# The first two rows of wo loaded by three DMAs over 100, 20 and 8 partitions

## The chip, the cores and the metric

The kernel runs on one core of one Trainium2 chip. The metric is the device time of one execution in microseconds, as the median over several runs. The inputs lie in HBM; a core has five engines (TensorE, called PE in the profile, VectorE or DVE, ScalarE or ACT, GpSimd or POOL, and SyncE or SP), an on-chip memory of 128 partitions, and 16 DMA engines, which carry every load.

## The reference

The reference mixes two branches for four tokens (B = 4, one position each) by a gate.

```python
g = _sigmoid((x * gate_w).sum(-1, keepdims=True))        # x: 4 x 1 x 512
# branch A: attention over the last 4096 of 16384 cached positions
q = (x @ wq) as 32 heads of 128
scores = einsum(q, k) * 128 ** -0.5                      # 8 key heads, each used by 4 query heads
p = softmax(scores)
a = einsum(p, v).reshape(B, 1, 4096) @ wo                # wo: 4096 x 512
# branch B: a gated unit
b = einsum(relu(x @ W_gate) * (x @ W_up), W_down)        # 512 x 1792, 512 x 1792, 1792 x 512
out = g * a + (1 - g) * b
```

All inputs are bf16. Keys and values of the window are 8 sets of 4 MB each, wq and wo 4 MB each, and the three matrices of branch B 1.75 MB each.

## The kernel before

The kernel doesn't call its engines one by one. It first collects, in a `Program` (lines 28 to 172), a list of operations for each engine, each with the names of the operations that it waits for, and then emits each list in the order in which it was collected. `Program.dma` (line 56) adds a DMA: unless a semaphore is named, each DMA gets one of its own, and its event is the count 16 on it. An operation waits for an event by waiting until the semaphore has reached the event's count.

Nearly all loads are issued by SP, in one queue and in this order: wq (line 568), then the key sets and value sets in turn (`load_k` at line 263, `load_v` at line 267), the two matrices W_gate and W_up (lines 279 and 280), the last value set, W_down (line 282), and last wo (lines 284 to 289). ACT issues two tiny loads at the start, x and gate_w (lines 273 and 274): they go to 16 and 4 partitions of the tile `xs`, and both have an outermost size of 4 in the source.

wo is seen as 128 partitions x 32 rows x 512 columns: a partition holds 32 consecutive rows of wo, 1 KB each. It goes to the tile `Wo`, which is another view of the memory `KT` that holds the transposed keys; so its DMAs wait for the last matmul that reads the keys, `("SC", NSET - 1, 1)`. `WO_CUTS = (0, 18, 26, 30, 32)` (line 23) cuts the 32 rows of a partition into four pieces of 18, 8, 4 and 2 rows, that is 2304, 1024, 512 and 256 KB, each loaded over all 128 partitions by one DMA with a semaphore of its own, `("WO", k)`.

The attention runs over 8 sets (a token and half of its key heads each), in a loop that PE executes once a set: scores, the maximum, the exponent, a permutation, the transposition of the weights, and the product with the values. Branch B's products are done in the last turn. Behind the loop stands the tail (lines 514 to 556):

- 14 matmuls of the "grouped" kind (`grouped`, line 516) multiply branch B's hidden values with W_down. They work in four groups of 32 PE columns in turn and add up into the tile `SB`.
- The last set's attention output is normalised and transposed; in the meantime PE does 4 and then 8 matmuls whose result nobody reads (`unread`, line 523, `IDLE = (4, 8)`).
- The rows 0 to 17 of each partition of wo (`GROUPED = 18`) go through 18 more grouped matmuls (line 533), each waiting for its piece of wo and for the attention output `oq`. ACT copies the sum to `part` (line 536).
- The rows 18 to 31 go through four matmuls each, one for a quarter of the columns (line 540), into the tile `AB`; each waits for its piece. After the first of these pieces, the matmuls of line 549 add `part` in.
- DVE and ACT copy the quarters to `outr` (line 554), and SP stores the result (line 574).

Of the kernel before, what the change touches and what calls it, by code (L numbers as in the profile page):

```python
# [15 lines left out]
NSET = 8  # L16
# [3 lines left out]
FAR = 1.0e9  # L20
LOWEST = -3.0e38

WO_CUTS = (0, 18, 26, 30, 32)
IDLE = (4, 8)
GROUPED = 18

# [148 lines left out]
def bass_gated_mix__sliding_block_cached__glu_gated_reglu__decode_kernel(  # L175
# [13 lines left out]
    with ExitStack() as ctx:  # L189
        def sb(name, shape, dt):  # L190
            return ctx.enter_context(nc.sbuf_tensor(name, shape, dt))
# [33 lines left out]
        p = sb("p", [128, 512], BF16)  # L225
# [26 lines left out]
        Wo = KT[:, :].bitcast(BF16).rearrange("p (i w) -> p i w", w=512)  # L252
# [3 lines left out]
        P = Program()  # L256
# [25 lines left out]
        P.dma("sp", lambda e: e.dma_start(Wd[:, :, :].rearrange("p i w -> p (i w)"),  # L282
                                          B_W_down.rearrange("(p i) w -> p (i w)", p=128)), ("WD",))
        wo_src = A_wo.rearrange("(p i) w -> p i w", p=128)
        for k in range(len(WO_CUTS) - 1):
            lo, hi = WO_CUTS[k], WO_CUTS[k + 1]
            P.dma("sp", lambda e, lo=lo, hi=hi: e.dma_start(  # L287
                Wo[:, lo:hi, :].rearrange("p i w -> p (i w)"),
                wo_src[:, lo:hi, :].rearrange("p i w -> p (i w)")), ("WO", k), [("SC", NSET - 1, 1)])

        P.op("pool", lambda e: e.memset(xz[:, :, :].rearrange("p t w -> p (t w)"), 0.0), ("XZ0",))
        P.op("pool", lambda e: e.memset(onesf[:, :], 1.0), ("ONESF",))
# [223 lines left out]
        def grouped(n, stat, mov, waits):  # L516
            g = n % 4
            P.op("pe", lambda e: e.matmul(SB[32 * g:32 * g + 32, :], stat, mov, start=(n < 4), stop=(n >= total - 4),
                                          tile_position=(0, 32 * g)), ("GR",) if n == total - 1 else None, waits)
# [13 lines left out]
        for i in range(GROUPED):  # L533
            k = max(k for k in range(len(WO_CUTS)) if WO_CUTS[k] <= i)
            grouped(NFT + i, oq[:, i:i + 31 * 32 + 1:32], Wo[:, i, :], [("WO", k), ("OQ",)])
        P.op("act", lambda e: e.copy(part[:, :], SB[:, :]), ("PART",), [("GR",)], sem="va")
        def quarter(q):
            return AB[32 * q:32 * q + 4, 128 * q:128 * q + 128]

        for k in range(1, len(WO_CUTS) - 1):  # L540
            for i in range(WO_CUTS[k], WO_CUTS[k + 1]):
                for q in range(4):
                    P.op("pe", lambda e, i=i, q=q: e.matmul(  # L543
                        quarter(q), oq[:, i:i + 97:32], Wo[:, i, 128 * q:128 * q + 128],
                        start=(i == GROUPED), stop=(i == 31), tile_position=(0, 32 * q)),
                        ("ACC",) if (i == 31 and q == 3) else None, [("WO", k), ("OQ",)])
            if k == 1:
                for q in range(4):
                    P.op("pe", lambda e, q=q: e.matmul(quarter(q), S32[:, 0:4], part[:, 128 * q:128 * q + 128],
                                                       start=False, stop=False, tile_position=(0, 32 * q)), None,  # L550
                         [("PART",), ("S32",)])
        for q in range(4):
# [3 lines left out]
                sem="fin" if q % 2 else None)  # L556
# [63 lines left out]
```

## Time and profile before

| what | value |
|---|---|
| median of 3 runs | 196.72 us (196.71 to 197.96) |
| the profiled execution's own time | 197.05 us |
| its span, first to last instruction | 195.5 us |
| mean granted TensorE clock | 0.769 |
| read from HBM | 81.01 MB, 414 GB/s over the span |
| the four pieces of wo, issue to landing | 20.8, 22.9, 23.6, 23.8 us |

The profile is that of one execution, and its times are microseconds from the start of the span. The 40 digits of a slice row are tenths of busy time in 40 equal slices of the span, some 4.9 us each; the DMA row is the mean over the 16 DMA engines. The chain is the work that ended last, followed back from the last instruction: "DMA KT<-in_A_wo_dram" is a time in which the chain waited for that load. In a timeline a line is: start, duration, engine, line of the kernel, operation, what it writes and reads, how many, and in brackets the idle time of its engine before and what ended that. In the view by windows a row is: the stretch, its length, the busy time of each engine with the number of instructions, the granted clock, the busy share of the DMA engines, and GB/s. "SPq" is the queue of DMAs that SP issues. In the rows for DMA queues, q1 is SP's queue and q10 is ACT's; each has its number of packets, MB, and share of the 16 engines' time.

### The profile page before, as it was taken

How to read it: one execution, taken by the hardware profiler on the slowest of the kernel's cores; microseconds unless marked ns; L12 is line 12 of the kernel's file. 1: busy time of each engine (PE TensorE's matmuls, PEld its weight loads, DVE VectorE, ACT ScalarE, POOL GpSimd, SP SyncE). 2: the span in 40 equal slices, each digit the busy share in tenths (PEclk: the TensorE clock that was granted, in tenths of full speed). 3: DMA queues.
4: the chain of work that ended last, by engine and by line, in shares of the span. 5: the costliest groups of instructions: out<-in, count | busy, mean ns of one | idle time of the engine just before them, and what ended most of it. 6: DMA issues, size and time to landing. Idle time of an engine off the chain costs nothing.

```text
span 195.5 us, 2431 instructions
## 1 busy us (share of the span) xinstructions
PE 94.6 (48%) x1017; PEld 45.0 (23%) x1017; DVE 116.7 (60%) x122; ACT 31.7 (16%) x51; POOL 15.3 (8%) x54
## 2 busy tenths in 40 slices
PE   0007525619630961196119621961196029684683
PEld 0002101106200620161016101610161015123231
DVE  0010299699399539943995399449944994264301
ACT  2002360140140014001400140014001400140011
POOL 7007010100100010001000100010001000000000
PEclk9999999966955599559757955695559658859788
DMA  6999999999999999999999999999999999999990
GB/s 215 426 443 442 436 436 449 442 429 429 436 436 429 429 429 429 442 429 429 436 429 429 429 429 429 429 429 429 429 429 429 429 422 425 440 429 425 424 381 12
DMA packets 3495, 81.04 MB, mean 414 GB/s; under 512 B 417, under 2 KB 421, under 8 KB 677
## 3 DMA queue, kind: packets, MB, share of 16 engines
q1 hardware_dynamic: 3464, 81.01, 96.8%
q8 instruction: 1, 0.02, 0.0%
q14 instruction: 2, 0.01, 0.0%
q10 hardware_dynamic: 28, 0.01, 0.0%
HBM read 81.01 MB, written 0.00 MB: 414 GB/s over the span
## 4 chain that ended last, share of the span: by engine, by line
DMA 79%; PE 17%; issue 1%; SPq 1%; ACTq 1%; DVE 0%; DVEq 0%
DMA Vsb<-in_A_v_cache_dram 61%; PE OB L427 13%; DMA KT<-in_A_wo_dram 12%; DMA xs<-in_gate_w_dram 6%; PE SB L385 2%; PE PB L344 2%; SPq L287 1%; ACTq L273 1%; PE FO L331 0%; DVEq L569 0%; DVE xz L324 0%; PE AB L543 0%; DVE zz L326 0%; DVE zr L329 0%; DVE xs L272 0%
## 5 line engine op out<-in xcount | busy, mean ns | idle before, releaser
L377 DVE STREAM_TRANSPOSE KT<-Ksb 128x4096 f32<-128x4096 f32 x16 | 70.9, 4434 | 3.7 <-DMA Ksb<-in_A_k_cache_dram 3.6
L427 PE MATMUL OB<-Vsb,pT 128*32 128x256 bf16 x512 | 26.7, 396 | 54.9 <-DMA Vsb<-in_A_v_cache_dram 54.9
L385 PE MATMUL SB<-KT,qS 128*32 128x512 bf16 x256 | 32.4, 659 | 6.1 <-DVE KT L377 6.1
L427 PEld LDWEIGHTS OB<-Vsb,pT 128*32 128x32 bf16 x512 | 20.4, 137 | 61.1 <-issue 50.2
L403 ACT ACTIVATE p<-SB,negmax 128x512 bf16<-128x512 f32 x8 | 5.5, 687 | 112.1 <-DVE negmax L397 112.1
L418 DVE STREAM_TRANSPOSE pT<-pP 128x1024 bf16<-128x1024 bf16 x16 | 18.7, 1205 | 3.7 <-ACT pP L411 3.7
L411 ACT ACTIVATE pP<-PB 128x1024 bf16<-128x1024 f32 x16 | 16.2, 1020 | 10.7 <-PE PB L406 10.7
L393 DVE TENSOR_REDUCE mx<-SB 128x1 f32<-128x512 f32 x8 | 5.5, 692 | 20.5 <-PE SB L385 20.5
L371 POOL COPY qS<-qT 32x64 bf16<-32x64 bf16 x32 | 7.4, 231 | 123.3 <-PE SB L385 116.0
L385 PEld LDWEIGHTS SB<-KT,qS 128*32 128x32 bf16 x256 | 10.7, 144 | 22.3 <-issue 11.9
L406 PE MATMUL PB<-p,perm 128*128 128x512 bf16 x32 | 10.0, 442 | 8.9 <-ACT p L403 8.9
L436 DVE TENSOR_TENSOR osb<-OB,emask 128x256 f32<-128x256 f32 x8 | 3.4, 424 | 10.4 <-PE OB L427 10.4
L360 DVE STREAM_TRANSPOSE qT<-Wff 128x1024 f32<-128x1024 f32 x2 | 2.5, 1225 | 8.8 <-ACT Wff L355 8.8
L324 DVE STREAM_TRANSPOSE xz<-xs 128x128 bf16<-128x128 bf16 x1 | 0.3, 311 | 12.3 <-DMA xs<-in_gate_w_dram 12.3
L331 PE MATMUL FO<-zr,onesf 128*128 128x4 f32 x2 | 0.6, 365 | 14.2 <-DVE zr L329 14.2
L395 PE MATMUL FO<-identw,mx 128*128 128x128 f32 x16 | 4.2, 346 | 6.4 <-DVE mx L393 6.4
L395 PEld LDWEIGHTS FO<-identw,mx 128*128 128x128 f32 x16 | 2.6, 203 | 14.2 <-DVE mx L393 14.2
L406 PEld LDWEIGHTS PB<-p,perm 128*128 128x128 bf16 x32 | 2.6, 103 | 12.7 <-ACT p L403 10.5
L397 DVE CUSTOM_DVE_ANT_0 mrow<-FO,qmask 128x128 f32<-128x128 f32 x8 | 2.3, 292 | 4.9 <-PE FO L395 4.9
L351 PE MATMUL PB<-Wff,rall 128*128 128x512 bf16 x8 | 3.8, 628 | 3.1 <-ACT Wff L355 2.0
L443 PE MATMUL FO<-osum,S 128*16 128x129 f32 x18 | 4.4, 338 | 0.0
L355 ACT CAST Wff<-PB 128x2048 bf16<-128x2048 f32 x2 | 3.7, 1866 | 4.0 <-PE PB L351 4.0
(71 smaller groups left out, 59.7 us busy)
## 6 DMA issues: line engine op xcount, KB each, us to landing
Ksb<-in_A_k_cache_dram SPq DMA_DIRECT2D x8, 4096.0 KB, 24.8
Vsb<-in_A_v_cache_dram SPq DMA_DIRECT2D x8, 4096.0 KB, 15.7
Vsb<-in_A_wq_dram SPq DMA_DIRECT2D x1, 4096.0 KB, 13.6
KT<-in_A_wo_dram SPq DMA_DIRECT2D x1, 2304.0 KB, 20.8
Wff<-in_B_W_gate_dram SPq DMA_DIRECT2D x1, 1792.0 KB, 19.4
Wff<-in_B_W_up_dram SPq DMA_DIRECT2D x1, 1792.0 KB, 23.0
Wd<-in_B_W_down_dram SPq DMA_DIRECT2D x1, 1792.0 KB, 18.5
KT<-in_A_wo_dram SPq DMA_DIRECT2D x1, 1024.0 KB, 22.9
```

Source lines behind the costliest of these rows:

```text
L344: P.op("pe", lambda e, half=half, t=t, g=g, col=col: e.matmul(PB[32 * g:32 * g + 32, 512 * half:512 * half + 512], xT[:, t, :], Vsb[:, col ...
L371: P.op("pool", lambda e, src=src, dst=dst: e.tensor_copy(dst, src[:, :, :, 8 * b, :]), ("QS", s, a), [("QT", half), ("QS", s, a - 1) if a ...
L377: P.op("dve", lambda e: e.transpose(Kn[:, 1024 * u:1024 * u + 1024], Kw[:, s % 2, lo:lo + 4096]), ("KTC", s, u), [("K", s), ("SC", s - 1, ...
L385: P.op("pe", lambda e, u=u, vo=vo, h=h: e.matmul(SB[32 * h:32 * h + 32, :], qS[:, 16 - 16 * u:48 - 16 * u, 4 * h + vo], Kt[:, h // 2, h % ...
L393: P.op("dve", lambda e: e.tensor_reduce(mx[:, :], SB[:, :], AXIS.X, ALU.max), ("MX", s), [("SC", s, 1)], sem="vd")
L395: P.op("pe", lambda e: e.matmul(FO[:, 128:256], mx[:, 0:1].to_broadcast([128, 128]), identw[:, :], start=True, stop=True), ("MT", s), [("M ...
L403: P.op("act", lambda e: e.activation(p[:, :], SB[:, :], ACTF.Exp, bias=negmax[:, par:par + 1], scale=SCALE), ("EXP", s), [("NEGMAX", s)], ...
L406: P.op("pe", lambda e, h=h: e.matmul(PB[:, 512 * h:512 * h + 512], perm[:, h, :], p[:, :], start=True, stop=True), ("PERM", s) if h == 3 e ...
L411: P.op("act", lambda e, k=k: e.activation(pP[:, 1024 * k:1024 * k + 1024].rearrange("p (c r h) -> p c r h", r=8, h=4), PB[:, :].rearrange( ...
L418: P.op("dve", lambda e, k=k: e.transpose(pT[:, :].rearrange("p (u c q) -> p c u q", u=2, c=64)[:, 32 * k:32 * k + 32], pP[:, 1024 * k:1024 ...
L427: P.op("pe", lambda e, g=g, blk=blk, n=n: e.matmul(OB[32 * g:32 * g + 32, 0:256], pT[:, 32 * blk:32 * blk + 32], Vsb[:, 256 * blk:256 * bl ...
L443: P.op("pe", lambda e: e.matmul(FO[0:16, 256:385], S16[:, :], osum[:, :], start=True, stop=True), ("SEL", s), [("OSB", s), ("S16",)])
```

## The change

The pieces of wo become five: the first, of 18 rows, is cut into 2 and 16. The new first piece (rows 0 and 1 of each partition, 2 KB a partition, 256 KB in all) is loaded by three DMAs, over the partitions 0 to 99, 100 to 119 and 120 to 127. The three count on one semaphore, "shares", and the event `("WO", 0)` is its count 48. The other four pieces are loaded as before, over 128 partitions each. The order of wo's bytes in the queue is otherwise kept, and every DMA of wo waits for the same matmul as before.

In the tail the same matmuls are done in the same order. The first two of the 18 grouped ones now wait for the new first piece, and the other sixteen for the second; the pieces of the four-quarter matmuls have their numbers moved up by one.

```diff
-WO_CUTS = (0, 18, 26, 30, 32)
+WO_CUTS = (0, 2, 18, 26, 30, 32)
+SHARES = (0, 100, 120, 128)
...
-        for k in range(len(WO_CUTS) - 1):
+        def load_wo(k, first, last, name, sem=None):
             lo, hi = WO_CUTS[k], WO_CUTS[k + 1]
-            P.dma("sp", lambda e, lo=lo, hi=hi: e.dma_start(
-                Wo[:, lo:hi, :].rearrange("p i w -> p (i w)"),
-                wo_src[:, lo:hi, :].rearrange("p i w -> p (i w)")), ("WO", k), [("SC", NSET - 1, 1)])
+            P.dma("sp", lambda e: e.dma_start(
+                Wo[first:last, lo:hi, :].rearrange("p i w -> p (i w)"),
+                wo_src[first:last, lo:hi, :].rearrange("p i w -> p (i w)")), name, [("SC", NSET - 1, 1)], sem=sem)
+
+        for n in range(len(SHARES) - 1):
+            load_wo(0, SHARES[n], SHARES[n + 1], ("WO", 0, n), "shares")
+        P.events[("WO", 0)] = ("shares", 16 * (len(SHARES) - 1), None, 0)
+        for k in range(1, len(WO_CUTS) - 1):
+            load_wo(k, 0, 128, ("WO", k))
...
-        for k in range(1, len(WO_CUTS) - 1):
+        for k in range(2, len(WO_CUTS) - 1):
...
-            if k == 1:
+            if k == 2:
```

## Prediction

> **What bounds the kernel now.** I read the page first: its busy shares, its slices and its chain.
>
> ```profile
> span 195.5 us, 2431 instructions
> PE 94.6 (48%) x1017; PEld 45.0 (23%) x1017; DVE 116.7 (60%) x122; ACT 31.7 (16%) x51; POOL 15.3 (8%) x54
> DMA  6999999999999999999999999999999999999990
> GB/s 215 426 443 442 436 436 449 442 429 429 436 436 429 429 429 429 442 429 429 436 429 429 429 429 429 429 429 429 429 429 429 429 422 425 440 429 425 424 381 12
> DMA 79%; PE 17%; issue 1%; SPq 1%; ACTq 1%; DVE 0%; DVEq 0%
> ```
>
> No compute engine is busy for more than 60% of the span, while the DMA row stands at 9 from the second slice to the last but one, at 422 to 449 GB/s. The kernel is a stream of loads, and its time is the moment at which the last load lands plus what comes behind it. So I looked at the end of the chain, in order of time, and at the timeline of the last microseconds.
>
> ```profile
> 168.79 23.80 DMA KT<-in_A_wo_dram
> 192.59 0.04 issue
> 192.63 0.32 PE AB L543 x8
> 192.95 0.02 issue
> 192.97 0.07 DVE outr L554
> ```
>
> The fourth and last piece of wo is issued at 168.79 and lands at 192.59. Behind it stand eight matmuls, the eviction and the store. Whatever the change does has to move that landing, or what stands behind it.
>
> ```profile
> 186.15 2.36 PE L525 MATMUL OB<-p,perm 128*128 128x512 bf16 x8
> 188.44 1.30 PE L518 MATMUL SB<-KT,oq 128*32 128x512 bf16 x18
> 189.78 0.59 ACT L536 COPY Ksb<-SB 128x512 f32<-128x512 f32 x1 [13.44 <-PE SB L518]
> 190.76 0.62 PE L543 MATMUL AB<-KT,oq 128*4 128x128 bf16 x32 [1.02 <-DMA KT<-in_A_wo_dram]
> 191.21 0.39 PE L549 MATMUL AB<-Ksb,S 128*4 128x128 f32 x8
> 191.99 0.40 PE L543 MATMUL AB<-KT,oq 128*4 128x128 bf16 x16 [0.40 <-DMA KT<-in_A_wo_dram]
> 192.63 0.29 PE L543 MATMUL AB<-KT,oq 128*4 128x128 bf16 x8 [0.24 <-DMA KT<-in_A_wo_dram]
> ```
>
> Each L543 group starts when its piece has landed. From 190.76 to 191.99 is 1.23 us for 512 KB, and from 191.99 to 192.63 is 0.64 us for 256 KB. A piece of 256 KB has 128 rows (partitions) of 2 KB; over 16 DMA engines that is 8 rows each, so one engine needs 0.64 / 8 = 0.08 us for a 2 KB row. This is my unit price.
>
> The view by windows shows who does that work at the end.
>
> ```profile
> 180.00:188.00 8.00, 5.73 (x48) 2.60 (x38) 2.10 (x6) 0.00 (x0) 0.00 (x0) 0.79 0.99 422
> 190.00:190.80 0.80, 0.04 (x4) 0.05 (x8) 0.00 (x0) 0.37 (x1) 0.00 (x0) 1.00 0.63 236
> 190.80:192.16 1.36, 0.96 (x52) 0.67 (x56) 0.00 (x0) 0.00 (x0) 0.00 (x0) 1.00 0.07 26
> 192.16:193.00 0.84, 0.52 (x24) 0.15 (x12) 0.03 (x1) 0.03 (x1) 0.00 (x0) 1.00 0.00 0
> ```
>
> The last two numbers of a row are the busy share of the 16 DMA engines and GB/s. Up to 188 all are busy (0.99, 422 GB/s). From 190.80 to 192.16 the share is 0.07, about one sixteenth, and 26 GB/s is one sixteenth of 422. So **one engine is late by some 1.36 us**, and it alone sets the end: the other fifteen have that much slack. No view says which of the sixteen it is.
>
> **The change part by part.** *Issue.* Four DMAs become seven, so SP issues three more.
>
> ```profile
> L287 SPq DMA_DIRECT2D KT<-in_A_wo_dram x4: 327/432/432, 167.5 to 168.8; - x4
> DMA to landing us min/median/max: 20.8/23.3/23.8
> SPq L574 <- DVE outr L554: 24.3, 1, 24.3
> ```
>
> 3 x 0.43 = 1.30 us more on SP, so the last issue ends near 170.5 instead of 169.2. The pieces wait in the queue behind loads issued before, for 20.8 to 23.8 us, and behind them SP only waits 24.3 us for the output. That backlog hides it: zero. Were it gone, 1.30 us would be on the path.
>
> *Packets.* The same 4 MB in 128 more rows. A KB costs 1.23 / 8 / 4 = 38.4 ns in the third piece's rows of 4 KB and 0.64 / 8 / 2 = 40 ns in rows of 2 KB, so shorter rows cost about 3 ns each here: 13 x 3 = 0.04 us on an engine, and nothing on one that gets none.
>
> *Shares.* This is the point of the sum. How a DMA is split can be counted from the queue rows.
>
> ```profile
> q1 hardware_dynamic: 3464, 81.01, 96.8%
> q10 hardware_dynamic: 28, 0.01, 0.0%
> ```
>
> q10 has the two loads into xs, of 16 and 4 rows: 28 - 20 = 8 packets are no data, 4 for each. q1 has 24 loads of 128 rows and the output's 4 rows: 3464 - 3076 = 388 = 24 x 16 + 4. I read that as one closing packet for each engine taking part: a DMA of 128 rows uses 16 engines, one whose outer size is 4 uses 4. Equal shares over the largest divisor up to 16 fit both. By this 100 rows go to 10 engines (10 each), 20 to 10 (2 each), 8 to 8 (1 each). If these start from the same end of the row of engines, eight engines get 13 rows of rows 0 and 1, two get 12, six get none, in place of 8 for each. Against 8 rows: +5 x 0.08 = +0.40 us, +4 x 0.08 = +0.32 us, and -8 x 0.08 = -0.64 us. [...]
>
> If the late engine is among the six, its work is 0.64 us less. Whether it ends 0.64 us earlier hangs on what limits its 26 GB/s. Alone at the end it moves no faster than beside fifteen others, so the limit is not shared by all; it is its own, or that of the eight partitions that it writes. Here the rows can't decide, and the cost is bounded from both sides: with a limit of its own, -0.64; with one of its partitions, the eight rows that it is spared are still written there, by others, while it works on wd or wo, and take 8 x 0.08 = 0.64 from it: 0. I take **0**: for the gain two things must hold (spared, and limited by itself), and in the other reading the rows are still on the late engine's partitions. [...]
>
> With that limit the loaded engines write beside the owners of the partitions, at worst at half speed: 13 x 0.16 - 8 x 0.08 = +1.44 us, 12 rows +1.28. Their slack is 1.36, so in the first case they would end at most 0.08 behind the late engine: still about 0.
>
> *PE's tail.* The first two grouped matmuls wait for rows 0 and 1, the other sixteen for the next piece, one wait more. Before, the group ran from 188.44 to 189.74, behind the L525 fillers that end at 186.15 + 2.36 = 188.51; its copy ends at 189.78 + 0.59 = 190.37, and the next piece lands at 190.76. 0.39 us of cover; nothing is gained by two matmuls that could start earlier, since the fillers stand ahead of them. If landings came 0.64 earlier, the 8 matmuls of L549 would be ready for the third piece still (190.37 + 0.4 = 190.8 against 191.35).
>
> **Sum.** 0 (issue) + 0.0 (packets) + 0 (late engine: -0.64 + 0.64) + 0 (tail) = 0. The profiled execution took 197.05 us, 195.5 of them its span; it is 0.33 above the median of the three runs, 196.72. I predict **196.7**; this case's own range is 196.4 to 197.0 (0.08 of overrun, and part of the 0.64 either way).
>
> **The rivals.**
> - *It works:* the late engine is spared and its rate is its own. Landing at 192.59 - 0.64 = 191.95, the loaded ones at 190.80 + 0.40 = 191.20 are no bound: 196.72 - 0.64 = 196.1. For it: the 0.07 row shows one engine late with all others idle, just what such a split can mend. Against it: both conditions are needed, and six of sixteen is less than half.
> - *It ends slower:* the late engine is one of the ten loaded ones. It decides as soon as that engine gets more than 8 rows. Price: +0.32 to +0.40 if its rate is its own, up to 13 x 0.16 - 0.64 = +1.44 if it shares every destination with a busy owner: 197.0 to 198.2, its middle 197.6. For it: ten of sixteen. Against it: the rows below.
>
> ```profile
> 2.39 10.97 DMA xs<-in_gate_w_dram
> Vsb<-in_A_wq_dram SPq DMA_DIRECT2D x1, 4096.0 KB, 13.6
> 0.80 0.40 SPq L568 DMA_DIRECT2D Vsb<-in_A_wq_dram  x1
> ```
>
> gate_w, on four engines, had landed by 2.39 + 10.97 = 13.36, while wq landed at 0.80 + 13.6 = 14.4. If the lag is already there, the four engines of gate_w don't have it; they are of the loaded kind, and the odds become six spared against six loaded.
> - *The split is not what I count:* the 100 rows go to fewer engines. On four, 25 + 5 + 2 = 32 rows of 0.08 stand against 8: +1.92 us, less the slack of 1.36 where the late engine isn't among them, more on fewer engines: 197.3 to 198.7 and up. Only q10's DMAs speak for it, and those have an outer size of 4.
>
> **How the numbers follow.** Forecast (the end stays within 0.3 us) 0.45; it works 0.20; late engine loaded 0.30; coarser split 0.05. Spared is some 0.6 by the above, and of that the limit of the partitions gets two thirds and over. The range goes from 196.0 (the gain, a little more) to 198.2 (the loaded engine's worst), which leaves some 0.1 outside. A measurement of this kernel can tell about 1% from no change, that is 1.97 us: every case but the last lies within. Faster 0.02, same 0.93, slower 0.05.
>
> **What would show it.** Issue: L287 x7, the last before 171. Shares: q1 with 128 + 28 = 156 more packets (3620). The late engine: a stretch of share 0.07 before the last landing; if it works, it shrinks from 1.36 to about 0.3 and the last L543 starts near 192.0; if the late engine is loaded, it grows, and the start goes to 193.0 or later; in my forecast the start stays near 192.6, while the share before it rises from 0.07 because loaded engines end later. I'm wrong if the last L543 moves by over 0.3 us, or if the output's store behind it takes another time.

## The result, and the profile after

| | before | after |
|---|---|---|
| median of 20 runs each | 196.75 us (196.49 to 197.96) | 197.48 us (196.78 to 199.82) |
| ratio after / before | | 1.0037, 95% interval 1.0020 to 1.0054 |
| the profiled execution: time, span | 197.05, 195.5 us | 197.14, 195.9 us |
| spans | 195.0 to 195.9 us, median 195.4 (131 runs, those beside the experiments) | 195.5 to 197.3 us, median 196.0 (19 runs) |

One of the 20 runs after, of 199.82 us, fell in a slower state of the chip and is left out of the spans and of the ratio.

The change makes the kernel slower by 0.4%, some 0.7 us. The forecast was no change, 196.4 to 197.0 us; the measured 197.48 us lies above that and within the wide range, on the side of the rival that ends slower.

The page of the changed kernel shows first that the loads still fill the span, and second that they have become slower near the end: slices 37 and 38 have 394 and 371 GB/s, where they had 425 and 424, and what was not moved there is moved later, in slices 39 and 40 (396 and 65 for 381 and 12).

```profile
span 195.9 us, 2434 instructions
...
DMA  6999999999999999999999999999999999999991
GB/s 227 426 429 428 442 448 442 428 435 442 435 442 428 428 428 435 428 428 428 428 428 428 428 428 428 435 428 435 428 428 428 428 422 432 444 419 394 371 396 65
...
q1 hardware_dynamic: 3620, 81.01, 97.2%
```

q1 has 156 packets more, as counted in the prediction: 128 rows and 28 closing packets, which is what 10, 10 and 8 engines give. The closing packets can be counted in the trace too: 416 of 4 bytes in q1, where there were 388. SP's part is harmless, as forecast: seven issues, the last at 170.0, whose piece lands 22.9 us later.

```profile
L288 SPq DMA_DIRECT2D KT<-in_A_wo_dram x7: 287/364/442, 167.6 to 170.0; - x7
```

The end of the chain has the same links, 0.34 us later (192.93 for 192.59):

```profile
170.02 22.91 DMA KT<-in_A_wo_dram
192.93 0.04 issue
192.97 0.32 PE AB L550 x8
193.29 0.02 issue
193.31 0.07 DVE outr L561
```

The view by windows, first of the kernel before and then of the changed one (the last two numbers are the busy share of the DMA engines and GB/s), tells where it goes:

```profile
180.00:184.00 4.00, 1.73 (x36) 0.97 (x25) 0.85 (x2) 0.00 (x0) 0.00 (x0) 0.96 1.04 443
```

```profile
180.00:184.00 4.00, 2.06 (x48) 1.53 (x44) 0.85 (x2) 0.00 (x0) 0.00 (x0) 0.85 1.05 327
190.80:192.16 1.36, 0.84 (x40) 0.55 (x40) 0.00 (x0) 0.44 (x1) 0.00 (x0) 1.00 0.66 258
192.16:192.50 0.34, 0.15 (x12) 0.15 (x16) 0.00 (x0) 0.00 (x0) 0.00 (x0) 1.00 0.12 42
```

From 180 to 184, when the engines come to rows 0 and 1, they are as busy as before (1.05; a packet counts in the window in which it starts, so a share can exceed 1) and move a quarter less (327 for 443 GB/s). From 190.80 to 192.16, where one engine was left before (0.07), some ten are at work on average (0.66), and in the next 0.34 us about two (0.12). The long stretch of a lone engine is gone, and still the end is later.

PE's timeline gives the time at which wd landed; wd stands in the queue just ahead of rows 0 and 1, and PE starts behind the engine that ends it last: in the kernel before, fifteen engines had done their packets of wd by 181.01 us and one at 182.27, and PE started at 182.77. Before, then after:

```profile
182.77 1.13 PE L518 MATMUL SB<-Wd,hT 128*32 128x512 bf16 x14 [2.27 <-DMA Wd<-in_B_W_down_dram]
```

```profile
183.64 1.08 PE L525 MATMUL SB<-Wd,hT 128*32 128x512 bf16 x14 [1.94 <-DMA Wd<-in_B_W_down_dram]
...
189.31 1.30 PE L525 MATMUL SB<-KT,oq 128*32 128x512 bf16 x18
...
191.09 0.62 PE L550 MATMUL AB<-KT,oq 128*4 128x128 bf16 x32 [0.48 <-DMA KT<-in_A_wo_dram]
```

wd itself is loaded as before, yet it lands 0.87 us later: something that comes behind it in the queue slows it.

The trace also holds every DMA packet with its start, duration and size. It doesn't name the engine, but in the kernel before 2671 of the 2688 packets of 14 KB and over start within 4 ns of the end of another, which I take for the one before it on its engine, so an engine's packets can be followed by their times. This is what they show of the late engine, the one that ends wd last:

| the late engine | before | after |
|---|---|---|
| its last two packets of wd | 0.54, 0.54 us | 0.86, 1.01 us |
| end of wd (PE starts 0.5 to 0.6 us behind it) | 182.27 | 183.02 |
| end of its last packet | 192.16 | 192.44 |
| the other engines' last packets end | at some 190.3 to 190.9 | at 192.48 at the latest |

In the changed kernel its packets of wd are followed directly by the 16 KB rows of the second piece (the last ends at 183.02, the first 16 KB row starts at 183.02): the late engine is one of the six that are spared. While the three DMAs run, packets take up to about twice their time (1.01 for 0.54 us in wd, up to 1.11 for 0.62 in the 16 KB rows, up to 0.17 for 0.08 in the 2 KB rows).

### The profile page after: what moved, and what is told of

It reads as the page before. It is cut to its first block, busy times and chain, and to the rows that moved or that the text cites. A ratio compares the mean times of both kernels' runs of the same rounds, so it can differ in the third digit from the quotient of the medians.

```text
span 195.9 us, 2434 instructions
## 1 busy us (share of the span) xinstructions
PE 94.4 (48%) x1017; PEld 46.0 (24%) x1017; DVE 116.8 (60%) x122; ACT 31.6 (16%) x51; POOL 15.2 (8%) x54
## 4 chain that ended last, share of the span: by engine, by line
DMA 78%; PE 17%; SPq 1%; issue 1%; ACTq 1%; DVE 0%; DVEq 0%
DMA Vsb<-in_A_v_cache_dram 61%; PE OB L434 13%; DMA KT<-in_A_wo_dram 12%; DMA xs<-in_gate_w_dram 5%; PE SB L392 2%; PE PB L351 2%; SPq L288 1%; ACTq L274 1%; PE FO L338 0%; DVEq L576 0%; DVE xz L331 0%; PE AB L550 0%; DVE zz L333 0%; DVE zr L336 0%; DVE xs L273 0%
## 5 line engine op out<-in xcount | busy, mean ns | idle before, releaser
L434 PE MATMUL OB<-Vsb,pT 128*32 128x256 bf16 x512 | 28.1, 412 | 54.5 <-DMA Vsb<-in_A_v_cache_dram 54.5
L434 PEld LDWEIGHTS OB<-Vsb,pT 128*32 128x32 bf16 x512 | 21.7, 144 | 61.0 <-issue 54.0
L532 PE MATMUL OB<-p,perm 128*128 128x512 bf16 x12 | 4.3, 515 | 0.0
```

What stands on the lines that cost most here:

```text
L434: P.op("pe", lambda e, g=g, blk=blk, n=n: e.matmul(OB[32 * g:32 * g + 32, 0:256], pT[:, 32 * blk:32 * blk + 32], Vsb[:, 256 * blk:256 * bl ...
L532: P.op("pe", lambda e: e.matmul(OB[:, :], perm[:, 0, :], p[:, :], start=True, stop=True))
```

## The experiments

The theories: (1) the rate is limited at the destination, so rows that an engine writes into another's partitions slow both; (2) the rate is an engine's own, and only the unequal shares count; (3) the cost is that of the cut, or of more DMAs; later (4), PE's tail.

**The cut alone.** In the changed kernel:

```diff
-SHARES = (0, 100, 120, 128)
+SHARES = (0, 128)
```

> Rows 0 and 1 are cut off as in the changed kernel, but loaded by one DMA over all 128 partitions. If the cost of the change lies in the split over 100, 20 and 8 partitions (theory 1: rows written by engines that don't own the partitions collide with the owners; or theory 2: the late engine is among those that get more rows), this kernel stands within 0.3 us of the kernel before, and from 180 to 184 us the 16 DMA engines move over 400 GB/s. If the cost lies in the cut itself (theory 3: more DMAs, more rows, one more wait on PE), it is slower by about the 0.7 us that the change measured.

Measured: ratio 0.9999 (0.9983 to 1.0015), spans 195.3 to 195.8. wd's first matmul starts at 182.77, where it did before, and the engines move over 400 GB/s, as expected. The cut is free; the loss is in the split.

```profile
180.00:182.00 2.00, 1.72 (x43) 1.26 (x32) 0.23 (x1) 0.00 (x0) 0.00 (x0) 0.72 1.00 404
182.00:184.00 2.00, 1.23 (x16) 0.69 (x17) 0.61 (x2) 0.00 (x0) 0.00 (x0) 1.00 1.00 426
```

**Other destinations, equal shares.**

```diff
-WO_CUTS = (0, 2, 18, 26, 30, 32)
-SHARES = (0, 100, 120, 128)
+WO_CUTS = (0, 16, 18, 26, 30, 32)
+SHARES = (0, 64, 128)
```

> The rows 0 to 15 of each partition of wo (2048 KB) are loaded by two DMAs, over partitions 0 to 63 and 64 to 127. Equal shares give every one of the 16 engines 4 + 4 rows, so no engine gets more work than before; only the owner of a destination changes. Theory 1 (the destination limits): each half is written by 16 engines into the partitions of 8, at half the rate, and 2048 KB take some 10 us where they took 5: slower by 3 to 5 us. Theory 2 (an engine's own limit): same within 0.3 us.

Measured: 203.78 us, ratio 1.0345 (1.0318 to 1.0371), some 7 us. The window in which the two halves are loaded:

```profile
182.00:192.00 10.00, 5.74 (x29) 2.39 (x29) 1.82 (x6) 0.00 (x0) 0.00 (x0) 0.83 0.97 205
```

All engines are busy (0.97) at 205 GB/s, just under half of 422. By the split that the packet counts of q1 fit, no engine has more rows than before, so theory 2 has nothing to explain it with. The loss is above the 3 to 5 us expected; part of it stands behind the loads, where PE's granted clock was lower (from 196 to 198 it was 0.50, and the first 32 four-quarter matmuls took 1.03 us where they took 0.62 before).

The same at the change's own size (rows 0 and 1, `SHARES = (0, 64, 128)`):

> Rows 0 and 1 by two DMAs over partitions 0 to 63 and 64 to 127: 4 + 4 rows for each engine, no engine spared or loaded, 16 engines writing into the partitions of 8. It has the foreign destinations of the change without its unequal shares. The same with eight times the bytes cost 6.8 us. Theory 1: slower by 0.6 to 0.9 us. Theory 2: same within 0.2 us.

Measured: ratio 1.0075 (1.0048 to 1.0103), median span 196.6, 1.2 us over that of before and above the 0.6 to 0.9 us expected. The chain's last landing is at 170.52 + 23.15 = 193.67, 1.08 us later than before, where half speed for eight rows gives 0.64.

```profile
170.52 23.15 DMA KT<-in_A_wo_dram
```

**The same split, four times the bytes** (`WO_CUTS = (0, 8, 18, 26, 30, 32)`):

> The same split over 100, 20 and 8 partitions with rows of 8 KB (rows 0 to 7 of each partition) in place of 2 KB: four times the bytes. Theory 2 with the late engine spared: the late engine wins 2.56 us, the loaded ones lose 1.6 us against a slack of 1.36: slower by about 0.3 us; with the late engine loaded, slower by 1.6 us. Theory 1: the loaded engines lose up to 4 x 1.44 = 5.8 us, less 1.36 of slack: slower by 2.5 to 4.5 us, with the DMA engines busy (share 1.0) at 300 to 350 GB/s for some 8 us from 181 on.

Measured: 201.84 us, ratio 1.0280 (1.0234 to 1.0326), some 5 us: above both.

```profile
182.00:190.00 8.00, 5.74 (x29) 2.36 (x29) 1.78 (x6) 0.00 (x0) 0.00 (x0) 0.79 1.00 209
...
194.60:196.40 1.80, 0.60 (x24) 0.60 (x28) 0.00 (x0) 0.25 (x1) 0.00 (x0) 0.53 0.62 251
```

209 GB/s at full share while the split is on, below the 300 to 350 expected, and towards the end a share of 0.62: ten of sixteen engines still at work, six done. Here the loaded engines set the last landings; at the end PE's matmuls run at a granted clock of 0.53, as the row shows, and the first 30 four-quarter ones behind the landing take 1.03 us, where 32 took 0.62 before, which is part of the excess.

**Lower or upper partitions only.** Both leave the other half of rows 0 and 1 unloaded.

```diff
-SHARES = (0, 100, 120, 128)
+SHARES = (0, 50, 60, 64)        # the lower half
+SHARES = (64, 114, 124, 128)    # the upper half, another kernel
```

> Of the rows 0 and 1 of wo only the partitions 0 to 63 are loaded, by three DMAs over 50, 10 and 4 partitions; the partitions 64 to 127 of these two rows are left out. Six engines get no rows, the others 6 or 7 in place of 8. The late engine is one of the six. If it owns partitions of the upper half, nobody writes into its partitions here. Theory 1 (the destination limits): it ends 0.64 us earlier, the kernel is faster by about 0.6 us. Theory 2 (an engine's own limit): faster by 0.6 us too.

> The counterpart: only the partitions 64 to 127 of rows 0 and 1 are loaded, by three DMAs over 50, 10 and 4 partitions; the partitions 0 to 63 of these two rows are left out. Same engines, same bytes, same number of DMAs; other destinations. Theory 1, with the late engine owning partitions of the upper half: its 0.64 us come back as others' rows, the last landing stays within 0.3 us of the kernel before, and this kernel is slower than the one with the lower half by 0.5 us or more. Theory 2: faster than before by 0.6 us, as with the lower half.

Measured: lower 1.0008 (0.9988 to 1.0028), median span 195.35; upper 1.0023 (1.0008 to 1.0038), median span 195.9. Lower half, wd's first matmul and the last landing:

```profile
182.87 1.08 PE L525 MATMUL SB<-Wd,hT 128*32 128x512 bf16 x14 [0.97 <-DMA Wd<-in_B_W_down_dram]
```

```profile
169.84 22.27 DMA KT<-in_A_wo_dram
```

Upper half:

```profile
183.28 1.93 PE L525 MATMUL SB<-Wd,hT 128*32 128x512 bf16 x14 [1.32 <-DMA Wd<-in_B_W_down_dram]
```

```profile
169.90 22.61 DMA KT<-in_A_wo_dram
```

With the lower half the last landing is at 192.11, 0.48 us earlier than before. A loaded engine, with 6 or 7 rows for 8, could win 0.16 at most: the late engine is one of the spared. With the upper half, the same rows on the same engines, wd lands 0.51 us later than before (0.10 with the lower half) and the last piece at 192.51: nearly all of the gain is gone, by the destination alone. The 0.6 us faster that I expected of the lower half did not come out in the runs: their spans go from 194.8 to 196.1, and the medians are equal. The difference between the two kernels, 0.55 us in the median span, points the expected way, but the intervals of their ratios overlap; the two profiles carry this argument.

**Half the bytes** (`WO_CUTS = (0, 1, 18, 26, 30, 32)`):

> The split over 100, 20 and 8 partitions with rows of 1 KB (row 0 alone) in place of 2 KB: half the bytes. If the change is slower because the loaded engines overrun their slack of 1.36 us by collisions (they ended some 2.0 us later in the changed kernel), half of it, 1.0 us, stays within the slack, and the late engine keeps its end (-0.32 spared, +0.32 from others' rows): within 0.3 us of the kernel before. If the cost is proportional to the bytes split (late engine pays more than it is spared), slower by 0.3 to 0.4 us.

Measured: ratio 1.0017 (1.0003 to 1.0032), median span 195.6 (195.3 to 196.2). The excess, 0.06 to 0.6 us, is about half of the change's, but the interval holds both expectations: the run doesn't tell whether the loss goes with the bytes or begins only where the slack ends. In its profile the last landing is at 192.44, 0.15 us earlier than before.

```profile
169.91 22.53 DMA KT<-in_A_wo_dram
```

**The split behind all other loads.** The three DMAs load rows 30 and 31, after everything else:

```diff
-        for n in range(len(SHARES) - 1):
-            load_wo(0, SHARES[n], SHARES[n + 1], ("WO", 0, n), "shares")
...
+        for n in range(len(SHARES) - 1):
+            load_wo(4, SHARES[n], SHARES[n + 1], ("WO", 4, n), "shares")
```

> The three DMAs over 100, 20 and 8 partitions are moved to the last piece (rows 30 and 31), behind all other loads; rows 0 and 1 are loaded over 128 partitions. The engines that own the partitions have then nothing left to write, the late one excepted. Theory 1: fewer collisions than in the changed kernel, the late engine keeps its end (-0.64 spared, +0.64 from others' rows): within 0.4 us of the kernel before, and faster than the changed kernel. Theory 2 with the late engine spared: faster than before by 0.6 us; with the late engine loaded: slower by 0.4 us.

Measured: ratio 1.0037 (1.0022 to 1.0052), some 0.7 us: not faster than the changed kernel, and not within the 0.4 us that theory 1 gave it. Its median span is 196.25; the profile is of a shorter one (195.9).

```profile
168.87 23.75 DMA KT<-in_A_wo_dram
192.62 0.04 issue
192.67 0.54 PE AB L550 x24
```

The landing that the chain waits for is at 192.62, where it was before (192.59): the late engine's end is kept, although it is spared eight rows. Its packets show how: its last 4 KB rows, written while the others' rows come in, took up to 0.44 us in place of 0.16, and it ended at 192.08, where it ended at 192.16 before. As the last two pieces come together, 24 matmuls stand behind it in place of 8 (0.54 for 0.32 us).

**Three DMAs without collisions, and three tiny ones.** Rows 0 and 1 cut by columns (512, 256 and 256 elements), each DMA over all 128 partitions:

> Rows 0 and 1 by three DMAs, as in the changed kernel, but cut by columns (512, 256 and 256 elements a partition), each over all 128 partitions: every engine gets 8 rows of each and writes its own partitions. The same number of DMAs on SP, more packets than in the changed kernel (384 in place of 128 data packets), no foreign destinations, no unequal shares. Theory 1: within 0.2 us of the kernel before. If part of the 0.7 us is the price of two or three more DMAs as such (theory 3 in a second form), slower by 0.2 to 0.5 us.

Measured: ratio 1.0029 (1.0011 to 1.0047), against theory 1. The last landing, though, is at 170.29 + 22.37 = 192.66, the median span 195.55, 0.15 us over that of before. What is larger is the time around the span: 2.1 to 2.5 us in 5 of the 12 runs, as against 1.2 to 1.5 in the others and over 1.7 in 1 of the 23 runs of the kernel before beside it.

```profile
170.29 22.37 DMA KT<-in_A_wo_dram
```

Then the kernel before with three more DMAs of 8 KB:

```diff
+            if k == 0:
+                for n in range(3):
+                    P.dma("sp", lambda e, n=n: e.dma_start(spare[0:16, n, :], wo_src[0:16, 0, 0:256]), ("SPARE", n), sem="spare")
```

> The kernel before with three more DMAs on SP behind wo's first piece, each of 16 rows of 512 B (8 KB) into a spare tile that nobody reads; seven DMAs of that group in all, as in the changed kernel, none split unequally. The loads end at most 0.1 us later. Theory 1 (collisions are the whole loss): within 0.15 us of the kernel before. Theory 3b (the three more DMAs of SP's program cost some 0.4 to 0.7 us in the median, behind the span, as the kernel cut by columns showed): slower by 0.3 to 0.7 us, its runs in two groups some 0.9 us apart.

Measured: ratio 1.0006 (0.9989 to 1.0024), median span 195.6, one run in 12 with over 1.7 us around it. The number of DMAs on SP is not the price, so theory 3b falls. Why the kernel cut by columns had five such runs stays open; in the changed kernel it was 2 of 19, in the kernel before 15 of 131.

**The changed kernel again.**

> The changed kernel once more, unaltered, for a second profile beside the kernels above. Slower than before by 0.5 to 1.0 us in the median of the runs. If the loss is collisions, whose order in time differs from run to run, its last wo piece lands at another time than 192.93 in this profile, and its runs spread over more than those of the kernel before; if the loss were a fixed price, landing and spread would repeat within 0.1 us.

Measured: ratio 1.0028 (1.0008 to 1.0048), spans 195.4 to 197.2; the median of the runs is 0.4 us over that of before, a little less than expected. The last landing is at 170.13 + 22.61 = 192.74, not 192.93, and wd's first matmul starts at 183.52. The spread is twice that of the kernel before, as collisions would have it; the 0.19 us between the two landings alone would say little, since the spans of the kernel before differ by up to 0.9 us too.

```profile
170.13 22.61 DMA KT<-in_A_wo_dram
```

```profile
183.52 1.93 PE L525 MATMUL SB<-Wd,hT 128*32 128x512 bf16 x14 [1.35 <-DMA Wd<-in_B_W_down_dram]
...
190.91 0.62 PE L550 MATMUL AB<-KT,oq 128*4 128x128 bf16 x32
```

Here the first L550 group starts without any idle time: PE's tail, which starts with wd, has no cover left.

The late engine again goes from wd (end 183.00) directly to the 16 KB rows, with five others. It ends its last packet at 192.31, 0.28 us after every other engine. From 190.80 to 192.16 some eight engines are at work on average (0.53), and behind that it works alone (0.01).

```profile
190.80:192.16 1.36, 1.06 (x44) 0.56 (x42) 0.00 (x0) 0.59 (x1) 0.00 (x0) 1.00 0.53 205
192.16:193.00 0.84, 0.61 (x24) 0.32 (x24) 0.00 (x0) 0.00 (x0) 0.00 (x0) 1.00 0.01 2
```

**The split with fewer pieces behind it.** `WO_CUTS = (0, 2, 26, 32)`, with the split and, as a control, with `SHARES = (0, 128)`:

> The change's split of rows 0 and 1 over 100, 20 and 8 partitions, with the rest of wo in two pieces (rows 2 to 25 and 26 to 31) in place of four: five DMAs, one more than before, which alone cost nothing. PE has 24 matmuls behind the last landing in place of 8, some 0.2 us. Compared with the next kernel, which has the same pieces without the split: theory 1 has this one slower by 0.2 to 0.5 us (the landing at 192.7 to 192.9 in place of 192.6); theory 3b alone has both the same.

> The counterpart: rows 0 and 1, rows 2 to 25, rows 26 to 31, each by one DMA over 128 partitions; three DMAs. Last landing at 192.6 to 192.7, the 24 matmuls behind it cost 0.2 us: slower than before by 0.1 to 0.3 us by either theory, its runs in one group.

Measured: 1.0074 (1.0042 to 1.0106) with the split, 1.0040 (1.0018 to 1.0063) without. The control misses its expectation. Its timeline shows why:

```profile
190.67 1.09 PE L525 MATMUL SB<-KT,oq 128*32 128x512 bf16 x16 [1.87 <-DMA KT<-in_A_wo_dram]
```

The grouped matmuls wait for rows 2 to 25 until 190.67, and PE's tail sets the end; its spans lie in two groups (195.6 to 195.9, 196.6 to 197.1). The intervals overlap; the pair does not settle what it was made for.

**PE's tail.** In the changed kernel, in the kernel before, and in the kernel with the split at the end:

```diff
-IDLE = (4, 8)
+IDLE = (4, 4)
```

> The changed kernel with 4 of the second 8 unread matmuls on PE left out (4 + 4 in place of 4 + 8). They stand on PE between wd's landing, which the split puts off by 0.75 to 0.86 us, and the grouped matmuls. Theory 4 (the split's loss is in part PE's tail: started later, it has no cover left, and runs in which PE is granted half its clock end 1 us later): spans draw together, to 195.4 to 196.1 with none over 196.6, and their median is at most 0.3 us over that of the kernel before; the time is slower by 0.0 to 0.2%. Theory 1 alone (the last landing varies with the collisions): spans as in the changed kernel, a median of 195.7 to 196.1 with a quarter of the runs over 196.6.

> The kernel before with the same 4 unread matmuls left out, the control of the kernel with fewer unread matmuls and the split. wd lands where it did, PE's tail has its cover: same within 0.15% by each theory, if the left-out matmuls don't matter to PE's clock.

> The split moved to the last piece, with the 4 unread matmuls left out. There the split comes behind wd, so wd's landing and the start of PE's tail stay where they were. Theory 4: leaving them out changes nothing (spans 195.5 to 196.8, slower than before by 0.2 to 0.5%), since here the loss is the last landing itself and the 24 matmuls behind it. If PE's tail were late here too, faster than the kernel with all of them by 0.3 us or more.

Measured: 1.0055 (1.0031 to 1.0078), 0.9990 (0.9969 to 1.0011) and 1.0043 (1.0022 to 1.0065). The first has its cover back (1.19 us idle, row below) and still spans from 195.5 to 197.1, seven of twelve from 196.4 up: that late start and lost cover alone make the executions long is not borne out. The second, the control, takes the same time as the kernel before, and the third spans 195.6 to 196.5; both are as theory 4 expected. Another form of it stays open: that in a long execution PE's tail runs at a lower granted clock. The kernel without the split above, whose end PE's tail sets, has two groups of spans 1 us apart, and in these profiles the granted clock stands at 0.54 to 0.61 in the changed kernel and in the kernel before from 184 to 188, and at 0.99 or 1.00 from 188 on. What it is in a long execution no profile shows.

```profile
190.97 0.62 PE L550 MATMUL AB<-KT,oq 128*4 128x128 bf16 x32 [1.19 <-DMA KT<-in_A_wo_dram]
```

The first of these kernels was profiled twice more, for a long execution:

> The changed kernel with 4 unread matmuls fewer, once more, for a profile of another execution: half of its executions had spans of 196.4 to 197.1 us, the one with a profile 195.6. In a long one, theory 1 (collisions at the destinations, other in each execution) has the last landing at 193.4 or later, later by as much as the span is longer; theory 4 (PE's tail) has the landing at 192.8 and the matmuls behind it at half the clock.

> The same once more, so that a long execution is likelier to be among the profiles: the same expectations.

Both were short ones (spans 195.9 and 195.8, last landings at 192.94 and 192.78).

## Why the prediction was wrong, point by point

- *What bounds the kernel:* right. One engine's lag sets the end, and the change acts there.
- *Issue, packets:* right. Three more issues are hidden, and the cut costs nothing (0.9999).
- *Shares:* right in the count: 156 packets more, some ten engines at work at the end of the fourfold split (a share of 0.62).
- *The late engine is spared:* right; only a spared engine can land 0.48 us earlier with the lower half, and the packets of both profiles show it. The lag is there from the first load on: in the kernel before, fifteen engines had done their last packet of wq by 12.79 and one at 13.99.
- *"If the late engine is among the six, ... I take 0":* this is the step that failed, by the size of a term. A limit at the partitions, and with it the +0.64, was my choice between two readings, and no run had shown it then. The runs showed its direction: with the same rows on the same engines, the last landing was at 192.11 with the lower half and at 192.51 with the upper, so the rows that the late engine is spared are still written into its partitions, and take time from it. But the two terms, -0.64 and +0.64, don't cancel. The packets show that it was spared 0.58 us (5.50 us for its eight rows of 18 KB before, 4.92 for eight of 16 KB in the kernel with the cut alone) and lost 0.86 us in the first profile (0.75 in wd, 0.11 in the rows behind it) and 0.73 us in the second. Net it ends 0.28 and 0.15 us later, and the last landing comes 0.34 and 0.15 us later. Why eight rows that take 0.64 us alone cost their owner 0.73 to 0.86 us stays open.
- *The slack of the loaded engines, "at most 0.08 behind the late engine":* right in both profiles. They work through the 1.36 us, as foreseen (0.66 and 0.53 of the engines where it was 0.07); the last of them ends 0.04 us behind the late engine in the first profile and 0.28 us before it in the second.
- *PE's tail:* the prediction gave it 0 and left out that the split meets wd, which stands ahead of it in the queue. PE's tail starts 0.75 to 0.87 us later, and in the second profile it has no cover left.
- *The sum:* 0, in place of a median span 0.6 us longer (0.25 in the second measurement). The profiles show 0.15 to 0.34 us of it, at the landing. By the prediction's own sign (the last group of matmuls moves by over 0.3 us) it is wrong in the first profile, with 192.97 for 192.63, and not in the second. The rest lies in executions with spans over 196.5 us, 9 of 31, which the kernel before doesn't have in 131. No profile caught one, and their cause stays open: collisions that fall worse and a PE tail at a lower clock are both argued, not shown.
- *The rivals:* "it ends slower" named the outcome, by the wrong engine: the late engine is not a loaded one. "It works" is refuted by the upper half: spared rows come back through the destination (wd 0.51 us later than before, the last landing 0.40 us later than with the lower half).

## What to carry to other kernels

Moving rows from a late DMA engine to others moved the source of the work here, not its destination: the rows taken off were written into the same partitions by others, and packets on both sides took longer (the late engine's last of wd 1.01 us for 0.54, the 2 KB rows up to 0.17 for 0.08). Before splitting a load over part of the partitions, ask which engines then write where, and price what such rows take from the owner at more than their own time: here 0.73 to 0.86 us for rows of 0.64 us. A lag of one engine at the end showed in the profile as a busy share near 1/16 (0.07 over 1.36 us), but not even the 0.64 us of the spared rows was to be had: the last landing came 0.15 to 0.34 us later.

## What the runs showed that I had not expected

The busy share did not tell contention here: it stood at 1.05 while the engines moved 327 GB/s, and at 0.97 at 205 GB/s, against 1.04 at 443 before. Share and GB/s together did. And collisions cost the engine that ends last more than the rows' own time: 1.08 us for 0.64 in the equal halves. The spans of the changed kernel spread over 1.9 us, where those of the kernel before spread over 0.9.
